# Four instead of six gate and value tiles of the first block in float32, and weight roundings on either engine

## The chip, the cores and the metric

The kernel runs on one core of a Trainium2 chip. The metric is the device time of one execution in microseconds (us). TensorE (PE) multiplies matrices, its weight loads are listed apart as PEld, VectorE is DVE, ScalarE is ACT, GpSimd is POOL, and SP issues the DMAs.

## The reference

A gated linear recurrence runs over 768 tokens of 4 batches with 8 heads of 32 columns (state 16). Its output, 3072 tokens by 256, goes through a gated layer of width 1536:

```python
y[:, :, sl] = y_intra + y_inter                      # chunks of 32 tokens
gate = 1.0 / (1.0 + np.exp(-(x @ w_gate)))           # 3072x256 @ 256x1536
val = x @ w_val
out = (gate * val @ w_out).astype(np.float32)
```

The three weights arrive as 64-bit floats; x, a, B and C as 32-bit floats.

## The kernel before

The tokens are worked on in six blocks of 512 columns (128 tokens of 4 batches). A block has the recurrence (`Scan`, for the first block `FirstUnit`, one unit for each of the 4 batches), then 12 gate and 12 value tiles of 128x512 (`gate`, `value`), then two projections (`proj`). Blocks 4 and 5 are multiplied together in a scheme with sums of operands (`unit`, `paired_proj`).

Weights come in 18 tiles w0 to w17. Even ones of w0 to w11 belong to gates, odd ones to values, each to two widths f: w0 and w1 to f = 0 and 1, w4 and w5 to f = 4 and 5. w12 to w17 are the output weights. `load_w` brings 128 x 1024 words (512 KB) of raw 64-bit floats. `split_w` makes 32-bit floats of them in five steps: a clip (L482, DVE or POOL), a scaled activation (L488, ACT), a shift (L490, DVE), a conversion (L495, ACT) and a sum (L497, POOL). After that the tile is "whole". `part_w` makes two parts of a whole tile: a rounded high part (L513, a copy on ACT) and the difference (L515, DVE or POOL). The parts are made one after the other in the list `order`, tiles that are not "plain" first.

A product in float32 (`thin`, L972) takes the whole weight and x as they are, with two matmuls. A product by parts (L981) takes six matmuls in the faster format, hi x hi, hi x lo and lo x hi for both halves of the contraction, and needs both parts of the weight and of x. The parts of x of the first block come from `parts_of_x` (L888 on ACT, L890 on DVE or POOL, for two halves of the columns). In the first block f = 0 is computed in halves of 256 columns (`halves_of`, L962, float32), f = 1 to 5 with whole 512 columns in float32, and f = 6 to 11 by parts.

The order of the work is written out. `run()` is a planner that runs while the kernel is built: it has one queue for each engine, a fixed cost for each step, the steps' needs, and `DUES`, a list of places: "gate0_1": "122 134" says that the first step of that task has place 122 of 1246 and its second place 134. A letter behind a place (a, d, p) fixes the engine ACT, DVE or POOL of a step that may run on two. Each engine then runs its steps in the planned order. Where the planner expects PE to be idle before 45 us it puts fillers ahead of a product (`keep_warm`, L289, small matmuls with no use): int(0.8 * idle / 0.22 + 0.4) of them. PSUM has three buffers "mm" that products take in turn (a product waits for the release of the third one before it), one "py" that the four first units share, and four banks of the recurrence.

The places of DUES that matter here:

| step | engine | before | after |
|---|---|---|---|
| loads w0, w1, w2, w3, w4 | SP | 3, 31, 43, 58, 76 | 32, 2, 63, 3, 56 |
| loads b0, b3, b1, b2 (B and C of a first unit) | SP | 2, 4, 5, 14 | 4, 5, 17, 24 |
| first transposes `products0_0` of unit 0 | PE | 8 | 23 |
| `spread0`, `spread3`, `spread1`, `spread2` (L741) | PE | 20, 10, 17, 33 | 8, 12, 16, 31 |
| weighing `result0_0` (L695) | DVE | 36 | 47 |
| `result0_2`, fourth step (L820) | PE | 100 | 106 |
| `xparts`, last step (L890) | DVE | 209 | 121 |
| `gate0_1` | PE | 122 | 127 |
| `part4` second step, `part5` second step | DVE | 351, 356 | 145, 185 |
| `gate0_4`, `value0_4` | PE | 168, 179 | 176, 190 |
| `part6` second step, `gate0_6` | DVE, PE | 206, 213 | 202, 212 |
| `part7` second step, `value0_6` | DVE, PE | 218, 223 | 216, 223 |
| `part8`, `gate0_8` | DVE, PE | 236, 240 | 236, 240 |
| `proj0_0` | PE | 283 | 282 |

Of the kernel before, what the change touches and what calls it, by code (L numbers as in the profile page):

```python
# [18 lines left out]
    "": "0 1", "b0": "2", "w0": "3", "b3": "4", "b1": "5", "products0": "6 7 9 13 18", "products0_0": "8 11 28",  # L19
    "spread3": "10 15", "split0": "12 16 19 24 32", "b2": "14", "spread1": "17 23", "spread0": "20 29", "x0": "21",  # L20
    "before0_0": "22p 27", "decays0_3": "25", "x1": "26", "products0_1": "30 34 42", "w1": "31", "spread2": "33 41",
    "x3": "35", "result0_0": "36 46 50 56 63 69", "decays0_0": "37p", "products0_3": "38 44 51", "x2": "39",
    "decays0_1": "40", "w2": "43", "before0_1": "45 47d", "products0_2": "48 55 64", "decays0_2": "49",
    "result0_1": "52 60 66 70 77 82", "early0_0": "53", "before0_3": "54p 57", "w3": "58",
    "result0_3": "59 78 87 91 95 98", "bq1_2": "61", "split1": "62 68 79 85 96", "r": "65", "before0_2": "67p 74p",
    "state0_0": "71", "w5": "72", "result0_2": "73 92 99 100 105 111", "early0_1": "75", "w4": "76",
    "xparts": "80 88d 116 209d", "bq1_0": "81", "half0_0": "83 103 112 117", "state0_1": "84", "w13": "86",
    "w6": "89", "early0_3": "90", "split2": "93 97 102 107 115", "bq1_3": "94", "early0_2": "101", "w7": "104",
    "state0_3": "106", "split3": "108d 119 124 126 139", "bq1_4": "109", "half0_1": "110 118 123 128",
    "state0_2": "113", "w9": "114", "w10": "120", "clip": "121 129 135", "gate0_1": "122 134",  # L30
    "split5": "125 131 136 142 164", "bq1_1": "127", "value0_1": "130 141", "bq1_6": "132",
    "split4": "133 137 143 146 156", "bq1_7": "138", "gate0_2": "140 151", "split13": "144d 150 154 158 177",
    "cq1_1": "145", "value0_2": "147 157", "ap": "148", "bq1_5": "149", "cq1_7": "152", "gate0_3": "153 162",
    "w8": "155", "cq1_4": "159", "split6": "160 165 169 172 183", "value0_3": "161 178",
    "split7": "163d 167 174 181 194", "p": "166", "gate0_4": "168 185", "w11": "170",
    "split9": "171d 175 191 197 233", "cq1_6": "173", "cq1_0": "176", "value0_4": "179 195", "cq1_5": "180",
    "turned1": "182 226", "w12": "184", "cq1_2": "186", "gate0_5": "187 201", "split10": "188 193 203 208 228",
    "cq1_3": "189", "part6": "190 206d", "z": "192", "p1_2": "196", "value0_5": "198 221", "w15": "199",
    "split8": "200d 204 212 216 222", "p1_0": "202", "w17": "205", "p1_3": "207", "w14": "210", "part7": "211 218d",
    "gate0_6": "213 225", "p1_1": "214", "split11": "215 219 238 242 245", "a1_1": "217", "a1_0": "220",  # L40
    "value0_6": "223 231", "bn1": "224", "x1_": "227", "part8": "229 236d", "gate0_7": "230 237",
    "masked1": "232 234", "value0_7": "235 246", "part9": "239 243d", "gate0_8": "240 250",
    "split12": "241d 244 249 253 265", "value0_8": "247 254", "part10": "248 252", "gate0_9": "251 259",
    "split17": "255 262 274 278 282", "value0_9": "256 264", "part11": "257 260d", "split15": "258d 275 284 289 296",
    "gate0_10": "261 268", "split14": "263d 266 270 272 277", "value0_10": "267 276 280d 322", "w16": "269",
    "early1": "271", "gate0_11": "273 281", "value0_11": "279 291 295d 316d",
    "proj0_0": "283 304 337 345 347 350 376", "part17": "285 292", "bq2_4": "286", "decays1": "287 299 300 305 311d",
    "bq2_0": "288", "bq2_6": "290", "bn2": "293", "bq2_2": "294", "part0": "297 308d",
    "proj0_1": "298 325 352 361 364 430 460", "a2_0": "301", "cq2_4": "302", "bq2_5": "303", "bq2_3": "306",
    "cq2_5": "307", "cq2_1": "309", "cq2_6": "310", "part1": "312 336d", "a2_1": "313",  # L50
    "split16": "314 317 320 323 328", "cq2_2": "315", "scan1": "318 332 335 340", "before1": "319d", "bq2_7": "321",
    "cq2_0": "324", "weigh1": "326 329 333 338 344 353 355 357 359", "bq2_1": "327", "cq2_3": "330", "cq2_7": "331",
    "bn3": "334", "part2": "339 341", "state1": "342 349d", "part3": "343 346d", "part4": "348 351d",
    "part5": "354 356d", "part12": "358 360p", "gate1_0": "362 370", "p2_0": "363", "p2_1": "365",
    "value1_0": "366 374 378a 382", "part13": "367 371d", "p2_3": "368", "p2_2": "369", "x2_": "372",
    "gate1_1": "373 381", "part14": "375 377p", "value1_1": "379 387 397 406d", "turned2": "380 384",
    "part15": "383 386", "gate1_2": "385 390", "masked2": "388 394", "value1_2": "389 396 400 426d",
    "decays2": "391 415 434 438 450", "part16": "392 399d", "gate1_3": "393 403", "early2": "395",
    "value1_3": "398 408 417a 422p", "a3_1": "401", "sums0": "402d 409 412p 428d 432p 433 470 482",
    "gate1_4": "404 413", "cq3_0": "405", "cq3_3": "407", "bq3_4": "410", "value1_4": "411 421 425d 445d",  # L60
    "cq3_4": "414", "bq3_0": "416", "gate1_5": "418 427", "bq3_7": "419", "a3_0": "420", "bq3_5": "423",
    "value1_5": "424 431 436 440p", "gate1_6": "429 437", "value1_6": "435 441 444a 499d", "gate1_7": "439 447",
    "value1_7": "442 451 454 462", "cq3_7": "443", "bq3_3": "446", "gate1_8": "448 458", "bq3_1": "449",
    "bq3_2": "452", "cq3_5": "453", "value1_8": "455 463 465a 472p", "before2": "456d", "bn4": "457",
    "decays3": "459 466 492 508 514p", "gate1_9": "461 467", "value1_9": "464 469 471 476",
    "scan2": "468 475 477 495", "gate1_10": "473 479", "weigh2": "474 481 483 488 500 511 513 516 520",
    "value1_10": "478 486 490a 496d", "bq3_6": "480", "gate1_11": "484 493", "cq3_2": "485", "cq3_1": "487",
    "cq3_6": "489", "value1_11": "491 497 501d 503p", "proj1_0": "494 509 517 531 534 561 657", "state2": "498 502d",
    "turned3": "504 515", "p3_0": "505", "p3_1": "506", "p3_3": "507", "x3_": "510", "p3_2": "512",
    "sums1": "518d 523d 524 526d 529d 532 535p 550", "masked3": "519 521", "a4_0": "522", "bq4_3": "525",  # L70
    "bq4_0": "527", "proj1_1": "528 548 560 566 568 593 623", "cq4_4": "530", "cq4_3": "533", "bq4_7": "536",
    "a4_1": "537", "bq4_1": "538", "gate2_0": "539 544", "early3": "540", "bq4_2": "541", "before3": "542p",
    "scan3": "543 549 551 553", "cq4_5": "545", "bq4_4": "546", "cq4_6": "547", "cq4_1": "552", "cq4_0": "554",
    "weigh3": "555 557 562 563 565 576 579 584 587", "state3": "556 559", "cq4_2": "558",
    "sums2": "564 567 569 571p 573p 578 582 592", "bq4_6": "570", "bq4_5": "572", "value2_0": "574 583 585d 589p",
    "cq4_7": "575", "bn5": "577", "p4_1": "580", "gate2_1": "581 588", "value2_1": "586 591 594 597",
    "gate2_2": "590 596", "value2_2": "595 599 600 606", "gate2_3": "598 603", "value2_3": "601 607 611 617p",
    "decays4": "602 622 641 661 671p", "p4_3": "604", "gate2_4": "605 614", "x4_": "608", "turned4": "609 615",
    "p4_2": "610", "value2_4": "612 618 625a 630", "sums3": "613p 627d 629 638d 646p 651 656p 673",
    "gate2_5": "616 624", "masked4": "619 620", "value2_5": "621 628 631a 634p", "gate2_6": "626 633",  # L80
    "value2_6": "632 636 639a 650", "gate2_7": "635 644", "bq5_3": "637", "cq5_5": "640",
    "value2_7": "642 649 653a 665d", "bq5_0": "643", "a5_0": "645", "gate2_8": "647 658", "bq5_2": "648",
    "p4_0": "652", "cq5_1": "654", "value2_8": "655 660 662 667", "gate2_9": "659 664",
    "value2_9": "663 668 669d 692", "gate2_10": "666 672", "value2_10": "670 678 681d 686p", "cq5_3": "674",
    "gate2_11": "675 684", "cq5_7": "676", "early4": "677", "cq5_0": "679", "before4": "680p", "bq5_4": "682",
# [1396 lines left out]
```

## Time and profile before

| | us |
|---|---|
| median of 3 runs | 345.24 (345.18 to 345.71) |
| the profiled execution | 345.54 |
| its span, first to last instruction | 343.7 |
| PE busy | 337.9 (98%) |
| DVE busy | 220.2 (64%) |
| POOL busy | 180.0 (52%) |
| ACT busy | 150.2 (44%) |

The profiled execution's time holds 1.84 us around its span. Matmuls are pipelined, and a duration in the trace overlaps the next one's start; the time that a product takes is read from start to start of successive products.

### The profile page before, as it was taken

To read this page: it belongs to the slowest core of one execution; us is meant where nothing else is said; L and a number is where in the kernel's file an instruction comes from. 1 tells how busy PE (TensorE), PEld (TensorE's weight loads), DVE (VectorE), ACT (ScalarE), POOL (GpSimd) and SP (SyncE) were. 2 spreads that over 40 slices of the span, in tenths; PEclk is the share of its full clock that TensorE was granted. 3 is DMA by queue.
4 is the path that set the end of the run, shared out by engine and by line. 5 is a ranking of instruction groups with operands and counts; after the bars stand their busy time and mean duration, and the time that the engine had idled before them with its cause. 6 is when DMAs were issued, how large, how long until landed. Compare 5 with 4: busy or idle time off the path is not lost.

```text
span 343.7 us, 7948 instructions
## 1 busy us (share of the span) xinstructions
PE 337.9 (98%) x3144; PEld 261.7 (76%) x3144; DVE 220.2 (64%) x377; ACT 150.2 (44%) x277; POOL 180.0 (52%) x181
## 2 busy tenths in 40 slices
PE   8899999999999999999999999999999999999996
PEld 3474587457888888888888888888888888888885
DVE  5889978956879872456666954566064646856221
ACT  4476987124744230136411513361047557645300
POOL 4646265431646434566774545489427885355500
PEclk9999999999999999999999999999999999999999
DMA  6996899871674376476543621108123733220032
GB/s 107 180 352 209 256 272 146 162 132 35 94 159 62 90 109 159 97 139 89 145 100 102 85 76 21 63 3 297 72 36 91 240 89 110 110 61 2 0 58 67
DMA packets 100247, 40.16 MB, mean 117 GB/s; under 512 B 88754, under 2 KB 91826, under 8 KB 99570
## 3 DMA queue, kind: packets, MB, share of 16 engines
q1 hardware_dynamic: 97906, 39.39, 49.3%
q10 hardware_dynamic: 2304, 0.26, 0.5%
q8 instruction: 25, 0.41, 0.5%
q14 instruction: 12, 0.10, 0.1%
HBM read 30.00 MB, written 9.63 MB: 115 GB/s over the span
## 4 chain that ended last, share of the span: by engine, by line
PE 98%; DVE 1%; ACT 0%; issue 0%
PE pg L981 17%; PE pv L981 17%; PE ux L1121 6%; PE acc L1121 6%; PE po L1017 5%; PE po L1013 5%; PE po L1019 5%; PE po L1018 5%; PE acc L1224 5%; PE uz L1121 5%; PE pg L972 2%; PE pv L972 2%; PE po L1251 2%; PE pcb L706 2%; PE pcb L691 2%; PE pcb L647 2%
## 5 line engine op out<-in xcount | busy, mean ns | idle before, releaser
L981 PE MATMUL pg<-xh,w 128*128 128x512 f32 x168 | 59.0, 392 | 0.0
L981 PE MATMUL pv<-xh,w 128*128 128x512 f32 x168 | 58.9, 391 | 0.0
L927 POOL TENSOR_TENSOR h<-g,h 128x512 fp32r<-128x512 f32 x27 | 38.3, 1420 | 24.4 <-ACT h L925 17.2
L921 DVE TENSOR_TENSOR g<-pv,g 128x512 f32<-128x512 f32 x38 | 26.1, 688 | 30.1 <-PE pv L981 29.1
L903 ACT ACTIVATE g<-pg 128x512 f32<-128x512 f32 x47 | 28.0, 596 | 39.4 <-PE pg L981 37.2
L981 PEld LDWEIGHTS pg<-xh,w 128*128 128x128 f32 x168 | 31.5, 188 | 6.7
L981 PEld LDWEIGHTS pv<-xh,w 128*128 128x128 f32 x168 | 31.5, 188 | 6.6
L497 POOL TENSOR_TENSOR wr<-wr 128x512 int32<-128x512 int32 x18 | 20.5, 1143 | 26.8 <-ACT wr L495 13.0
L981 PE MATMUL pg<-xl,w 128*128 128x512 f32 x84 | 32.7, 389 | 0.0
L981 PE MATMUL pv<-xl,w 128*128 128x512 f32 x84 | 32.7, 389 | 0.0
L1017 PE MATMUL po<-h,w 128*128 128x512 f32 x76 | 30.8, 405 | 0.0
L1019 PE MATMUL po<-h,w 128*128 128x512 f32 x76 | 29.6, 390 | 0.0
L1018 PE MATMUL po<-h,w 128*128 128x512 f32 x76 | 29.6, 389 | 0.0
L577 DVE TENSOR_TENSOR_SCAN ab<-ab,delta 128x512 f32<-128x512 f32 x20 | 28.1, 1424 | 0.0
L925 ACT CAST h<-g 128x512 fp32r<-128x512 f32 x26 | 16.0, 619 | 24.2 <-DVE g L921 24.0
L1048 POOL TENSOR_TENSOR c<-c,c 128x512 f32<-128x512 f32 x13 | 17.2, 1326 | 17.9 <-ACT c L1176 9.2
L1048 POOL TENSOR_TENSOR h<-c,h 128x512 fp32r<-128x512 f32 x16 | 21.0, 1323 | 9.4 <-ACT h L1200 9.3
L1048 POOL TENSOR_TENSOR sw<-sw 128x128 f32<-128x128 f32 x36 | 18.9, 535 | 11.2 <-DVE sw L1048 10.2
L1028 DVE STREAM_TRANSPOSE o<-po 128x256 f32<-128x256 f32 x16 | 6.3, 430 | 21.2 <-PE po L1019 19.2
L1200 ACT CAST h<-c 128x512 fp32r<-128x512 f32 x24 | 14.9, 619 | 10.7 <-POOL c L1048 7.1
L981 PEld LDWEIGHTS pv<-xl,w 128*128 128x128 f32 x84 | 15.8, 188 | 3.2
L981 PEld LDWEIGHTS pg<-xl,w 128*128 128x128 f32 x84 | 15.8, 188 | 3.2
(197 smaller groups left out, 733.2 us busy)
## 6 DMA issues: line engine op xcount, KB each, us to landing
w_s<-sp SPq DMA_DIRECT2D x12, 512.0 KB
s<-w_s SPq DMA_DIRECT2D x12, 512.0 KB
ab<-a_z SPq DMA_DIRECT2D x10, 512.0 KB
wr<-in_moe_w_gate_dram SPq DMA_DIRECT2D x6, 512.0 KB
wr<-in_moe_w_val_dram SPq DMA_DIRECT2D x6, 512.0 KB
wr<-in_moe_w_out_dram SPq DMA_DIRECT2D x6, 512.0 KB
xn<-in_x_dram SPq DMA_DIRECT2D x5, 512.0 KB
out_dram<-o SPq DMA_DIRECT2D x144, 16.0 KB
```

Source lines behind the costliest of these rows:

```text
L497: nc.gpsimd.tensor_tensor(out=lw.bitcast(I32), in0=hw.bitcast(I32), in1=lw.bitcast(I32), op=ALU.add)
L577: nc.vector.tensor_tensor_scan(out=t, data0=t, data1=delta.rearrange("p h l -> p (h l)"), initial=0.0, op0=ALU.mult, op1=ALU.add,)
L903: nc.scalar.activation(gs[k, f], pm, AF.Sigmoid)
L921: nc.vector.tensor_tensor(out=g, in0=pm, in1=g, op=ALU.mult)
L927: engines[eng].tensor_tensor(out=hl, in0=g, in1=hh.bitcast(F32), op=ALU.subtract)
L981: nc.tensor.matmul(pm, w[:, part, kt, fs], xx[:, kt], start=(i == 0), stop=(i == 3 * NK - 1))
L1013: nc.tensor.matmul(acc, whole[NF + f // 2][:, f % 2, ms], hs[k, f], start=start, stop=stop)
L1017: nc.tensor.matmul(acc, hi, hh, start=start, stop=False)
L1018: nc.tensor.matmul(acc, hi, hl, start=False, stop=False)
L1019: nc.tensor.matmul(acc, lo, hh, start=False, stop=stop)
L1048: engines[eng].tensor_tensor(out=out, in0=in0, in1=in1, op=op)
L1121: nc.tensor.matmul(out, a[i], b[j], start=start and n == 0, stop=n == 2, skip_group_check=True)
```

## The change

`NPLAIN` falls from 6 to 4: w4 and w5 are no longer plain, so f = 4 and 5 of the first block are multiplied by parts, like f = 6 to 11. Their parts are then made first in `order`, before the tiles of the first block that use them, and not after the first block as now. The rounding copies of `part_w` and of `weight_sums` (L513, L1065) may run on POOL as well as on ACT. All places of DUES are new, for the whole kernel.

```diff
 DUES = {
-    "": "0 1", "b0": "2", "w0": "3", "b3": "4", "b1": "5", "products0": "6 7 9 13 18", "products0_0": "8 11 28",
...
+    "": "0 1", "w1": "2", "w3": "3", "b0": "4", "b3": "5", "products0": "6 7 10 19 25", "spread0": "8 13",
+    "split1": "9 11 28 33 39", "spread3": "12 18", "split3": "14p 21 30 43 50", "x0": "15", "spread1": "16 22",
...
-    NPLAIN = 6
+    NPLAIN = 4
     NWHOLE = 10
...
-    copies = {"dve": nc.vector.tensor_copy, "act": nc.scalar.copy}
+    copies = {"dve": nc.vector.tensor_copy, "act": nc.scalar.copy, "pool": nc.gpsimd.tensor_copy}
...
-        yield step("act", ACT_SB, needs)
+        eng = yield step(("act", "pool"), (ACT_SB, 0.75), needs)
         hw, lw = halves.pop(i)
         hi, lo = parts_of(i)
-        nc.scalar.copy(hi, hw)
+        copies[eng](hi, hw)
...
-        yield step("act", ACT_SB)
+        eng = yield step(("act", "pool"), (ACT_SB, 0.7))
         parts = hp.tile([P, 2, 512], F32R, tag="r1", name=f"sp{i}")
-        nc.scalar.copy(parts[:, 0], t[:, 1])
+        copies[eng](parts[:, 0], t[:, 1])
```

## Rows read from the trace of the kernel before

**Rows 1.** Stretches: length, busy us of PE, PEld, DVE, ACT, POOL; clock, DMA, GB/s.
```profile
0.00:24.36 24.36, 21.75 (x336) 12.98 (x337) 18.03 (x44) 12.77 (x37) 12.23 (x27) 1.00 0.88 203
24.36:34.66 10.30, 10.30 (x25) 4.71 (x24) 9.54 (x14) 6.43 (x11) 6.33 (x7) 1.00 0.72 232
24.36:41.53 17.17, 17.17 (x42) 7.85 (x40) 15.96 (x29) 12.83 (x23) 8.41 (x9) 1.00 0.78 248
200.00:240.00 40.00, 40.00 (x445) 32.91 (x444) 23.12 (x35) 14.63 (x26) 27.08 (x26) 1.00 0.27 90
280.00:320.00 40.00, 40.00 (x179) 33.14 (x178) 25.90 (x40) 23.23 (x42) 21.96 (x20) 1.00 0.25 80
```

**Rows 2.** All waits of PE over the span: us in total, times, longest.
```profile
PE warm L237 <- DVE warm_sb L234: 1.1, 1, 1.1
PE py L706 <- ACT xw L834: 0.5, 1, 0.5
PE pcb L691 <- DVE m L695: 0.5, 1, 0.5
PE py L289 <- ACT xw L834: 0.3, 1, 0.3
PE mm L820 <- DVE sm L724: 0.2, 1, 0.2
```

**Rows 3.** Timeline of PE from 24 to 59 us: start, us, instruction.
```profile
24.36 1.88 PE L972 MATMUL pg<-xw,wr 128*128 128x512 f32 x4
41.53 0.83 PE L289 MATMUL pg<-eye 128*128 128x128 f32 x6
42.12 0.48 PE L981 MATMUL pg<-xh,w 128*128 128x512 f32 x1
43.59 0.38 PE L289 MATMUL pv<-eye 128*128 128x128 f32 x2
43.73 0.48 PE L981 MATMUL pv<-xh,w 128*128 128x512 f32 x1
45.20 0.40 PE L981 MATMUL pg<-xh,w 128*128 128x512 f32 x1
49.30 0.39 PE L981 MATMUL pv<-xh,w 128*128 128x512 f32 x1
58.83 10.46 PE L1013 MATMUL po<-h,wr 128*128 128x512 f32 x24
```

**Rows 4.** Timeline of DVE, 40 to 49 us: parts of weights (L515) and x (L890).
```profile
40.59 0.68 DVE L515 TENSOR_TENSOR w<-wr,w 128x512 fp32r<-128x512 f32 x1
41.19 0.68 DVE L890 TENSOR_TENSOR xl<-xw,xh 128x512 fp32r<-128x512 f32 x1
48.01 0.69 DVE L515 TENSOR_TENSOR w<-wr,w 128x512 fp32r<-128x512 f32 x1 [0.51 <-issue]
```

**Rows 5.** Timeline of PE, 5 to 25 us: transposes, visits, fillers, halves.
```profile
5.95 0.30 PE L756 MATMUL pt<-eye,bn 128*128 128x128 f32 x1
6.19 1.02 PE L741 MATMUL pa<-apart,of_unit 128*128 128x512 f32 x2
12.63 0.24 PE L706 MATMUL py<-m,xn 64*32 64x64 f32 x1
13.28 0.33 PE L756 MATMUL pt<-eye,bn 128*128 128x128 f32 x1
17.03 0.71 PE L289 MATMUL py<-eye 128*128 128x128 f32 x4 [0.27 <-ACT xw L834]
18.53 1.14 PE L962 MATMUL pgv<-xw,wr 128*128 128x256 f32 x4
19.60 0.45 PE L820 MATMUL mm<-cd,sm 128*64 128x64 f32 x8
20.64 0.71 PE L289 MATMUL mm<-eye 128*128 128x128 f32 x4
21.28 0.45 PE L820 MATMUL mm<-cd,sm 128*64 128x64 f32 x8
21.66 2.86 PE L962 MATMUL pgv<-xw,wr 128*128 128x256 f32 x12
```

**Rows 6.** Timeline of DVE, 6 to 30 us.
```profile
6.89 0.43 DVE L482 TENSOR_SCALAR wr<-wr 128x512 f32<-128x512 f32 x1 [1.98 <-DMA wr<-in_moe_w_gate_dram]
7.25 1.22 DVE L744 TENSOR_TENSOR_SCAN ab<-pa,delta 128x512 f32<-128x512 f32 x1
11.38 0.69 DVE L695 TENSOR_TENSOR m<-pcb,ab 128x512 f32<-128x512 f32 x1
25.74 1.26 DVE L482 TENSOR_SCALAR wr<-wr 128x512 f32<-128x512 f32 x1
29.37 2.59 DVE L1307 TENSOR_TENSOR_SCAN a<-a,az 32x768 f32<-32x768 f32 x1
```

**Rows 7.** SP: issue of the first weight load.
```profile
2.58 0.67 SPq L468 DMA_DIRECT2D wr<-in_moe_w_gate_dram  x1
```

**Rows 8.** Groups by line and shape, whole span.
```profile
L513 ACT CAST w<-wr 128x512 fp32r<-128x512 f32 x18 | 11.6, 658 | 4.9 <-DVE w L515 3.9 <-POOL w L515 1.0
L515 POOL TENSOR_TENSOR w<-wr,w 128x512 fp32r<-128x512 f32 x6 | 8.5, 1423 | 10.5 <-ACT w L513 10.5
L482 DVE TENSOR_SCALAR wr<-wr 128x512 f32<-128x512 f32 x18 | 10.6, 597 | 2.0 <-DMA wr<-in_moe_w_gate_dram 2.0
```

**Rows 9.** POOL at the start: the one copy of 128x512; and its sum at 25.61.
```profile
2.09 0.61 POOL L257 COPY delta<-eye 128x512 f32<-128x512 f32 x1 [0.78 <-DVE eye L255]
25.61 1.11 POOL L497 TENSOR_TENSOR wr<-wr 128x512 int32<-128x512 int32 x1
```

230 rows, old and new, of the table DUES are left out of this document.

## The prediction

> **What bounds the kernel now.** I read the stretches first, then the waits of PE, then its timeline. The stretches show PE busy from end to end behind 24.36 us (the reader sees the length and the busy time equal), and idle for 24.36 - 21.75 = 2.6 us before it; the granted clock is 1.00, the 2.4 GHz level, everywhere [rows 1]. The waits say the same from the other side: PE waited five times, 2.6 us together [rows 2]. So from the first float32 gate tile at 24.36 [rows 3] the program is one unbroken queue on PE. What shortens that queue shortens the kernel one for one as long as no operand comes late, and what moves its start moves the end. The other engines matter through operands that PE would wait for. They are tightest in the first block, where DVE is busy 9.54 of 10.30 us [rows 1].
>
> **The products.** The ten float32 products of f = 1 to 5 run from 24.36 to 41.53 [rows 3]: 1.717 us each. The last ten by parts run from 45.20 to 58.83 [rows 3]: 1.363 each. Four change kind: 4 x (1.363 - 1.717) = -1.42 us on PE.
>
> **The fillers at the seam.** Where PE goes over to parts it runs six fillers from 41.53 to 42.12 and two from 43.59 to 43.73 [rows 3], 0.59 + 0.14 = 0.73 us. They stand where the plan expected x's low part, which DVE ends at 41.87 [rows 4], and the parts of w7. After the change that step of x has place 121, ahead of the first gate. If the parts of w4 to w7 are on time no filler is needed: -0.73. If the plan expects as much idle time at the new seam they move there: 0. I take -0.73 and count late parts by themselves.
>
> **Parts earlier.** w4 and w5 get their parts ahead of gate0_4 and value0_4: for each an ACT copy of 0.66 us [rows 8] and a DVE difference of 0.68 [rows 4]. Behind the first block as much falls away, where nothing was late. With the gate at 24.36 the seam comes at 24.36 + 6 x 1.717 = 34.66 and gate0_6 at 34.66 + 4 x 1.363 = 40.11, against 42.12 now. So DVE must end w6's difference, now at 41.27 [rows 4], some 1.2 us earlier. Queued ahead of it on DVE from the first gate on are, if the flexible steps stay there: 2 differences and its own at 0.68, 12 clips and shifts at 0.42 (the short row [rows 6]) or 0.60 (the mean [rows 8]), four gate-value products at 0.69 (taken as the differences are), one scan over a at 2.59 [rows 6], and 0.8 for the halves: 13.2 or 15.4 us. The step of x, four of w13 and the transposes of chunk 1 now stand elsewhere. There are 40.11 - 24.36 = 15.75 us. DVE's own waits now take 17.17 - 15.96 = 1.2 us of this stretch [rows 1]. So PE stalls between 0 (13.2 + 1.2) and 0.9 (15.4 + 1.2 - 15.75). I take 0.4, about the middle. What is late next is w9: its difference ends at 48.70 [rows 4], value0_8, the first to use it, starts at 49.30 [rows 3], 0.6 us of slack at today's pace.
>
> **POOL as a place for roundings.** The trace has no rounding on POOL. From below its price is the one copy of this size, 0.61 us, from above POOL's difference with the same operands, 1.42; ACT needs 0.66 [rows 8, 9]. POOL was busy 8.41 of 17.17 us [rows 1] and has room. The other price is on DVE: a clip took 1.26 us while POOL's sum ran from 25.61 to 26.72, against 0.43 alone [rows 6, 9], so 0.8 us went to one POOL instruction. The copies without a fixed engine ahead of gate0_6 are three (w4, w5, w6). Three times 0.8 on DVE is 2.4; zero is the other end, if they stay on ACT or fall beside DVE work that reads PSUM. I take 0.2 for PE, near the lower end, as the rows above leave DVE some cover and ACT has the shorter queue. The Trainium skill, "SBUF — State Buffer", section "Who interferes with whom", says that DVE and GpSimd share a pair of ports under an exclusive lock and that the later one blocks fully; the long clip agrees with it. By that rule every rounding on POOL would stop a clip or shift for its whole length; this is the third rival.
>
> **The head.** The start of the queue is the other term, and the new places change it throughout. Now the transposes of unit 0 run at 5.95 and its weighing on DVE at 11.38 [rows 5, 6]. The new order loads w1 and w3 ahead of B and C and lets PE spread three units first. A scan begins 7.25 - 6.19 = 1.06 us after its spread [rows 5, 6], so the first at about 7.0; the transposes wait for a buffer "mm" that the second scan releases, 1.22 us each [rows 6]: 9.4. Behind them come ACT's copies, two more scans and a few short steps on DVE, and unit 0's weighing ends at about 13.9, 1.8 us later than now. By then the other units are further than now. What PE has left up to the first gate is four visits of 0.65 (12.63 to 13.28), four of 0.38 (21.28 to 21.66), halves of 1.07 and 2.70, and 1.2 for transposes and products of units 1 and 2 [rows 5]: 9.1 us. Now the same pieces take from 12.63 to 24.36, 11.7 us, with eight fillers and waits among them [rows 2, 5]. So the new first gate lies between 13.9 + 9.1 = 23.0 and 13.9 + 11.7 = 25.6, that is -1.4 to +1.2. I take 24.1, -0.3, just below the middle, since three units ready at once should need fewer waits.
>
> **Behind the first block** PE's work is the same piece for piece, and PE has no wait there now [rows 1, 2]. The order is new for every engine; I take 0, with a few tenths open either way.
>
> **Sum**, against the profiled execution's 345.54 us (span 343.7 and 1.84 around it): -1.42 - 0.73 + 0.4 + 0.2 - 0.3 = -1.85, so 343.7. The median of the runs lies 0.3 below that execution: 345.24 - 1.85 = 343.4.
>
> **Rivals.** (1) The weights keep their pace: parts come as late as now, and the queue gains only the least slack, 0.6 us at w9: 344.6. For it: DVE at 93% ahead of the seam [rows 1]. Against: x's late part has moved away, and POOL has room. (2) Slower, by a late start: B and C of every unit stand behind 1 MB of weights. The first weight load was issued at 2.58 and its clip began, when it had landed, at 6.89 [rows 6, 7], 4.3 us. If each of the two delays B and C by half of that, unit 0 is ready 4.3 us later than 5.95, 0.9 past the 9.4 at which its buffer is free, and x, with a third load ahead, up to another 1.0. With today's waits the gate then starts at 26.5 to 27.5. The other terms give -1.55, so it decides from 24.36 + 1.55 = 25.9 on; the time is 345.8 to 346.8, I say 346.4. For it: all of PE's waits are in the head now [rows 2]. Against: the loads land while DVE is at its scans. (3) POOL's roundings lock DVE: of the 2.4 us above, less the 0.6 already counted, 1.7 shows: 345.1. For it the long clip, against it that only three copies are free to move.
>
> **Chances.** Forecast 0.55 (its own range 342.3 to 344.3), rival 1 0.2, rival 2 0.15, rival 3 0.1. A measurement can tell from no change here about 0.2%, 0.7 us: faster is below 344.55, slower above 345.93. The forecast is all faster; rival 1 gives 0.12 faster and 0.08 same; rival 2 0.13 slower and 0.02 same; rival 3 0.02 faster, 0.06 same, 0.02 slower. Together 0.69, 0.16 and 0.15. The range runs from 342.0 (no stall, gate 1.1 early: -1.42 - 0.73 - 1.1 = -3.25) to 345.4, with rivals 1 and 3 in it; the late start is left out.
>
> **What would show it.** In the changed profile: six whole float32 products of 1.72 us and sixteen by parts of 1.36 in the first block; the first gate tile between 23.0 and 25.6; gate0_6 at about 40 without fillers ahead of it, or else a wait or fillers there (rival 1; with long clips beside copies on POOL, rival 3); the first projection at about 57 instead of 58.83 [rows 3]; no wait of PE behind that. A first gate behind 25.9 makes the prediction wrong, and so does any wait of PE behind 60 us that adds up to more than a microsecond.

## The result, and the profile after

| | before | after |
|---|---|---|
| median, us | 345.67 (22 runs, 345.18 to 345.97) | 347.84 (22 runs, 346.16 to 351.01) |
| ratio, with its 95% interval | | 1.0067 (1.0055 to 1.0078) |
| profiled execution; its span | 345.54; 343.7 | 348.59; 346.8 |
| first float32 gate | 24.36 | 27.29 |
| first gate to first projection | 34.47 | 34.13 |
| first projection to the end of the span | 284.87 | 285.38 |

The change makes the kernel 0.7% slower; forecast were 343.4 us and a range up to 345.4. Its executions also spread over 4.9 us, those of before over 0.8. Of the 3.1 us that the span gained, 2.93 lie ahead of the first gate, -0.34 between it and the first projection, 0.51 behind. The profiled execution after lies 0.75 us above its kernel's median, so the terms below add up to 3.1 us where the medians differ by 2.2. Ratios leave out executions more than 1.5% above the fastest of their kernel, which medians and ranges keep (one each of e3, e10 and e12). (Lines of the changed kernel are numbered one lower: L971 is L972 of before.)

The stretches of the kernel after, as in [rows 1]: length, busy us of PE, PEld, DVE, ACT, POOL, each with its rows, then the clock, DMA share and GB/s.

```profile
0.00:18.90 18.90, 17.15 (x219) 9.96 (x219) 14.00 (x32) 9.39 (x28) 12.15 (x26) 1.00 0.86 167
0.00:24.50 24.50, 21.90 (x344) 13.64 (x345) 17.79 (x45) 12.85 (x37) 12.78 (x26) 1.00 0.90 207
0.00:27.28 27.28, 24.05 (x354) 15.60 (x355) 20.08 (x48) 13.96 (x39) 14.20 (x27) 1.00 0.92 223
27.29:61.42 34.13, 33.84 (x134) 24.00 (x133) 27.82 (x49) 25.09 (x44) 15.29 (x16) 1.00 0.87 197
61.42:346.80 285.38, 282.22 (x2689) 226.78 (x2687) 170.37 (x278) 108.98 (x189) 158.60 (x145) 1.00 0.43 96
```

The same view of the kernel before, for the two stretches that [rows 1] does not have:

```profile
24.36:58.83 34.47, 34.47 (x122) 22.27 (x121) 30.17 (x56) 27.29 (x48) 17.72 (x18) 1.00 0.92 230
58.83:343.70 284.87, 281.68 (x2689) 226.42 (x2687) 171.98 (x279) 110.17 (x193) 150.05 (x137) 1.00 0.42 96
```

Keep the counts in mind: up to the first gate PE ran 354 matmul rows, 336 before [rows 1]. All waits of PE in the kernel after, which answer to [rows 2]:

```profile
PE pgv L961 <- issue: 1.4, 1, 1.4
PE warm L236 <- DVE warm_sb L233: 1.1, 1, 1.1
PE mm L819 <- issue: 0.6, 1, 0.6
PE pv L980 <- DVE w L514: 0.3, 1, 0.3
PE py L705 <- DVE m L694: 0.2, 1, 0.2
```

The two largest new ones name no operand: "issue". Where they lie is seen in PE's timeline of the kernel after (start, us, instruction, rows, idle time before it), to be read against [rows 3, 5]:

```profile
14.12 0.24 PE L705 MATMUL py<-m,xn 64*32 64x64 f32 x1 [0.21 <-DVE m L694]
15.93 0.71 PE L288 MATMUL py<-eye 128*128 128x128 f32 x4
17.63 0.49 PE L288 MATMUL mm<-eye 128*128 128x128 f32 x2
18.05 0.39 PE L819 MATMUL mm<-cd,sm 128*64 128x64 f32 x5
19.01 0.33 PE L819 MATMUL mm<-cd,sm 128*64 128x64 f32 x3 [0.58 <-issue]
19.93 0.71 PE L288 MATMUL mm<-eye 128*128 128x128 f32 x4
23.06 0.71 PE L961 MATMUL pgv<-xw,wr 128*128 128x256 f32 x2
25.14 2.32 PE L961 MATMUL pgv<-xw,wr 128*128 128x256 f32 x10 [1.37 <-issue]
27.29 1.02 PE L971 MATMUL pg<-xw,wr 128*128 128x512 f32 x2
38.98 1.05 PE L288 MATMUL pv<-eye 128*128 128x128 f32 x8
45.37 0.60 PE L288 MATMUL pv<-eye 128*128 128x128 f32 x4
```

The reader sees PE stop in the middle of a group of equal small products (after five of eight rows of L819) and between the two matmuls of one half product, which read the same two tiles. The stops stand at matmul rows 219 and 344 of the stretches above. At the seam there are now 12 rows of fillers (8 before), 0.81 + 0.36 = 1.17 us from start to next start.

### The profile page after: what moved, and what is told of

The parts are those of the page before. It is cut to its first block, busy times and chain, and to the rows that moved or that the text cites. A ratio compares the mean times of both kernels' runs of the same rounds, so it can differ in the third digit from the quotient of the medians.

```text
span 346.8 us, 8004 instructions
## 1 busy us (share of the span) xinstructions
PE 340.1 (98%) x3174; PEld 266.4 (77%) x3174; DVE 218.3 (63%) x375; ACT 148.0 (43%) x272; POOL 188.1 (54%) x188
## 4 chain that ended last, share of the span: by engine, by line
PE 97%; issue 1%; DVE 1%; ACT 0%; DVEq 0%
PE pg L980 17%; PE pv L980 17%; PE ux L1120 6%; PE acc L1120 5%; PE po L1016 5%; PE po L1012 5%; PE po L1018 5%; PE po L1017 5%; PE acc L1223 5%; PE uz L1120 5%; PE po L1250 2%; PE pcb L705 2%; PE pcb L690 2%; PE pcb L646 2%; PE pv L971 1%; PE pg L971 1%
## 5 line engine op out<-in xcount | busy, mean ns | idle before, releaser
L980 PE MATMUL pv<-xh,w 128*128 128x512 f32 x176 | 61.9, 392 | 0.3 <-DVE w L514 0.3
L980 PE MATMUL pg<-xh,w 128*128 128x512 f32 x176 | 62.1, 394 | 0.0
L926 POOL TENSOR_TENSOR h<-g,h 128x512 fp32r<-128x512 f32 x27 | 37.4, 1391 | 11.7 <-ACT h L924 9.3
L980 PEld LDWEIGHTS pv<-xh,w 128*128 128x128 f32 x176 | 33.0, 188 | 7.6 <-DVE w L514 0.7
L980 PEld LDWEIGHTS pg<-xh,w 128*128 128x128 f32 x176 | 33.0, 188 | 7.4 <-issue 0.2
L924 ACT CAST h<-g 128x512 fp32r<-128x512 f32 x33 | 20.4, 620 | 34.6 <-DVE g L920 34.5
L980 PE MATMUL pg<-xl,w 128*128 128x512 f32 x88 | 34.3, 390 | 0.0
L980 PE MATMUL pv<-xl,w 128*128 128x512 f32 x88 | 34.3, 389 | 0.0
L576 DVE TENSOR_TENSOR_SCAN ab<-ab,delta 128x512 f32<-128x512 f32 x20 | 29.4, 1474 | 0.0
L1047 POOL TENSOR_TENSOR c<-c,c 128x512 f32<-128x512 f32 x14 | 19.4, 1389 | 17.1 <-DVE c L1161 9.3
L1047 POOL TENSOR_TENSOR sw<-sw 128x128 f32<-128x128 f32 x33 | 16.6, 510 | 15.1 <-DVE sw L1047 14.6
```

The lines of the kernel that those rows point to most:

```text
L576: nc.vector.tensor_tensor_scan(out=t, data0=t, data1=delta.rearrange("p h l -> p (h l)"), initial=0.0, op0=ALU.mult, op1=ALU.add,)
L924: copies[eng](hh, g)
L926: engines[eng].tensor_tensor(out=hl, in0=g, in1=hh.bitcast(F32), op=ALU.subtract)
L980: nc.tensor.matmul(pm, w[:, part, kt, fs], xx[:, kt], start=(i == 0), stop=(i == 3 * NK - 1))
L1047: engines[eng].tensor_tensor(out=out, in0=in0, in1=in1, op=op)
```

## The experiments

Theory A is that the new order of the head costs the time: A1, PE's gaps belong to numbers of its instruction stream, where the next block of instructions isn't there yet; A2, operands are late there. Theory B is that the parts of the weights set the pace at the seam. Medians of before on the same chips were 345.26 (e1 to e4), 345.30 (e5 to e8), 345.43 (e9, e10), 345.33 (e11) and 345.52 (e12).

**One half of the order at a time.** e1 is the kernel before (six float32 tiles) with the new order up to the first gate; e2 the kernel after with the old one.

```diff
 DUES = {          # e1: in before.py
-    steps up to gate0_1 in the order of before
+    steps up to gate0_1 in the order of after, the rest as before
 DUES = {          # e2: in after.py
-    steps up to gate0_1 in the order of after
+    steps up to gate0_1 in the order of before, the rest as after
```

> The kernel before (six f in float32, roundings on ACT) with the changed kernel's order up to the first gate tile only; the old order from there on. Theory A (the loss is the head: PE's start of the queue comes about 3 us later): first gate at about 27.3 us as in the changed kernel, time before + 2.9 - 0.7 (no late parts at the seam, since the weights had longer) = about 347.8 us, with a spread of some us between runs. Theory B (the loss is at the seam, where parts by weights come late): no loss here, 345 us or less.

> The changed kernel (four f in float32) with the old order up to the first gate tile, the new order from there on. Theory B or the prediction's third step (parts of w4 to w7): the first gate is at 24.4 again. If parts are on time, 345.6 - 1.4 - 0.7 = 343.5 us. If the weights' pace is the bound, PE waits or runs fillers at the seam (f = 4 and 5) for about 3 to 4 us, the first projection is no earlier than 58.8, and the time is 346 to 347.5. Theory A alone (only the head was wrong) says 343.5 to 344.5.

e1 took 350.98, ratio 1.0163 (1.0146 to 1.0179); e2 348.18, 1.0079 (1.0064 to 1.0095). PE's timeline of e1, then of e2:

```profile
26.24 2.32 PE L961 MATMUL pgv<-xw,wr 128*128 128x256 f32 x10 [2.19 <-issue]
28.39 1.88 PE L971 MATMUL pg<-xw,wr 128*128 128x512 f32 x4
47.85 0.72 PE L980 MATMUL pg<-xh,w 128*128 128x512 f32 x2 [1.65 <-DVE w L514]
```
```profile
34.58 1.05 PE L288 MATMUL pg<-eye 128*128 128x128 f32 x8
36.87 2.62 PE L288 MATMUL pv<-eye 128*128 128x128 f32 x22
```

The new head brings the gap along into the old kernel, at the same product; the time is 3 us above what A said, with 2.1 us of waits for weights at the seam and the first gate 1.1 us later than A had it. With the old head the gap at the half product is gone (0.28 us are left at row 219) and the first gate is at 24.28. But of the 3.0 us saved there 2.1 go at the seam, with 30 rows of fillers (3.2 us from start to next start): the first projection is at 60.49, and the time 0.7 us above what B said.

**No fillers; other numbers of rows.** e3 is the kernel after without any filler. e4 (before) and e5 (after) have the same warm-up columns in eleven matmuls instead of three, 16 rows more. e6 drops after's fillers ahead of the first gate (13 matmuls, not 16) and puts 26 rows of 32 columns into the warm-up instead.

```diff
-FILL, MORE, FILL_T, COLD = 0.8, 0.4, 0.22, 45.0      # e3
+FILL, MORE, FILL_T, COLD = 0.0, 0.0, 0.22, 45.0
-WARM = (4, 4, 3)                                     # e4, e5
+WARM = (1, 1, 1, 1, 1, 1, 1, 1, 1, 1, 1)
-for _ in range(int(FILL * idle[0] / FILL_T + (0.9 if first_y[0] else MORE))):   # e6
+for _ in range(int(FILL * idle[0] / FILL_T + (0 if first_y[0] else MORE))):
-idle[0] = start - free["pe"] if eng == "pe" and start < COLD else 0.0      # e6
+idle[0] = start - free["pe"] if eng == "pe" and 27.0 < start < COLD else 0.0
+for _ in range(13):
+    nc.tensor.matmul(warm[:, :32], warm_sb, warm_sb[:, :32], start=True, stop=True)
```

> The changed kernel without any filler matmul. Theory A1 (PE's gaps in the head lie at fixed instruction numbers, 219 and 344 matmul rows, where the next block of instructions has not arrived): the 26 filler rows ahead of the second gap are gone, so that place moves into the float32 gates, where an instruction lasts 0.2 us, and the 1.4 us gap ahead of the halves goes; 1.5 to 2.5 us less than the changed kernel, about 345.5 to 346, and less spread. Theory A2 (the gaps are operands that come late): the gap stays at the halves, fillers turn into waits, 347 to 348 us.

> The kernel before with the same warm-up columns in 11 matmuls of 128 columns in place of 3 (16 more matmul rows and 16 more weight loads ahead of everything, nothing else). Theory A1: the block's end that fell at row 345, in the float32 gates, now falls at old row 329, among the halves of f = 0, after the fast small matmuls; a gap without a data wait appears there at about 22 to 24 us, the time rises by 0.3 to 1.5 us and its spread grows. Theory A2: no change, 345.6 within 0.3.

> The kernel after, with 16 more matmul rows in the warm-up, ahead of everything (the same columns cut into eleven short matmuls instead of three). Theory A1 (PE's gaps without a shown wait stand at numbers of its instruction stream, where the next block of instructions is not there yet): the gaps, now at matmul rows 219 and 344 from the start, stay at these numbers, so they move 16 rows back in the work: the first (0.58 us) out of the group L819 x5 into the products L690 ahead of it, the second (1.37 us) out of the second half product to just ahead of the first, at about 21.6. The time changes little (347 to 349) if their sizes stay. Theory A2 (an operand is late there): the gaps stay at the same instructions of the work, 0.58 inside L819 and 1.37 inside the second half product, and the time stays at 347.8.

> The kernel after without its 16 fillers ahead of the first gate, and with 13 matmuls of 32 columns in the warm-up, so that every piece of work from the second unit's visit on keeps its number in PE's stream to within a few rows; the fillers at the seam stay. Theory A1: the gaps come back at the same rows as in the kernel after (inside L819 and inside the second half product) though no filler is left; the first gate lies at 25.5 to 26.5, only the fillers' own time earlier than 27.29, and the time is 346.2 to 347.2. Theory F (the fillers themselves hold the head up, the gaps are a by-product of the time they take): no gaps above 0.5 us, first gate at 24.3 to 24.7 as without any filler, time 345.2 to 345.8.

e3 took 346.67, 1.0042 (1.0023 to 1.006): first gate 24.35, the gap at the halves gone, 328 rows ahead of the gate; the time is 0.7 us above what A1 said, and a gap of 1.00 us stands at row 1743. e4 took 345.89, 1.0023 (1.0011 to 1.0036): rise and spread (2.2 us) are as A1 said, but its profiled run, at 345.48 one of the fastest, does not show the gap. PE came to row 344 there at 22.66, just as its block was ready: its packet (such packets are shown below) ended at 21.24, 2.4 us sooner than in the kernel before. e5 took 354.48, 1.0274 (1.025 to 1.0297), and e6 352.64, 1.0214 (1.0182 to 1.0247). The sizes that I expected of e5 and e6 were far too small. The places were right, but for e6's second gap, which did not come. Stretches and timeline of e5:

```profile
0.00:17.60 17.60, 15.93 (x219) 11.32 (x220) 13.45 (x31) 8.92 (x28) 11.99 (x25) 1.00 0.85 168
0.00:24.00 24.00, 19.50 (x345) 14.10 (x346) 16.94 (x41) 11.40 (x34) 13.03 (x26) 1.00 0.85 199
24.60:28.60 4.00, 3.95 (x17) 2.69 (x17) 0.69 (x4) 0.99 (x3) 0.00 (x0) 0.57 1.06 359
18.00 0.45 PE L690 MATMUL pcb<-bct 32*64 32x128 f32 x9 [0.79 <-issue]
24.63 0.21 PE L715 MATMUL mm<-xn,bd 64*32 64x64 f32 x1 [3.06 <-issue]
```

With 16 rows put in at the start the gaps stay at rows 219 and 345 and so fall into other work: into the products L690 and into the last row of a visit. That is A1's forecast to the row, and A2 falls. Behind the 3.06 us the granted clock was 0.57 over 4 us, so mostly the 1.2 GHz level, which costs again. The first gate came at 30.48, 3.2 us later than in the kernel after. Behind the first projection e5 needs 288.1 us, 2.75 more than the kernel after; two later gaps make 2.5 of these:

```profile
84.61 0.27 PE L646 MATMUL pcb<-ct,sm 32*64 32x64 f32 x2 [1.54 <-issue]
202.77 0.50 PE L1017 MATMUL po<-h,w 128*128 128x512 f32 x1 [1.00 <-issue]
```

e6, its stretch up to the gap and the gap:

```profile
0.00:22.00 22.00, 17.49 (x218) 10.43 (x219) 14.23 (x32) 9.48 (x28) 12.94 (x26) 1.00 0.90 195
23.27 0.45 PE L821 MATMUL mm<-cd,sm 128*64 128x64 f32 x8 [3.08 <-issue]
```

Row 218, without a filler in sight. (The 26 small rows also delayed the first scans by 3.6 us, and behind the gap the clock was 0.60 over 4 us, so e6 says nothing on the fillers' own time.)

**What ends a gap.** The trace has a DMA queue of kind "instruction". The kernel after, 22.50 to 23.00 us, then the whole span (packets, MB, share of 16 engines):

```profile
q8 instruction: 1, 0.02, 13.9%
q8 instruction: 25, 0.41, 0.5%
```

Each of its packets has 0.41 MB / 25 = 16 KB; the one above took 0.139 x 16 x 0.5 = 1.11 us. Narrow stretches give each packet's start to 0.05 us, and every gap ends 1.3 to 1.5 us behind the end of one:

| kernel | matmul rows before the gap | packet starts, ends | PE goes on | behind it | gap |
|---|---|---|---|---|---|
| after | 219 | 16.05, 17.56 | 19.01 | 1.45 | 0.58 |
| after | 344 | 22.60, 23.71 | 25.14 | 1.43 | 1.37 |
| e1 | 344 | 23.85, 24.95 | 26.24 | 1.29 | 2.19 |
| e5 | 219 | 15.05, 16.54 | 18.00 | 1.46 | 0.79 |
| e5 | 345 | 22.10, 23.20 | 24.63 | 1.43 | 3.06 |
| e6 | 218 | 20.70, 21.92 | 23.27 | 1.35 | 3.08 |
| e9 (below) | 1744 | 159.50, 160.59 | 162.10 | 1.51 | 1.37 |

The other gaps without an operand that the traces show (of 0.28 to 1.65 us: one each in e2, e7, e10, e11 and e12, two in e3 and the two later ones of e5) end 1.4 to 1.6 us behind a packet too.

In the kernel before the packets start as late, at 15.25 and 22.55, and at row 219 PE waits only 0.1 us. But there PE has 336 rows ahead of the gate, and row 344 comes behind the second float32 product, at 24.36 + 2 x 1.717 = 27.8. The block is there at 23.65 + 1.4 = 25.1, and nothing waits. In the kernel after PE is at row 344 at 23.77 and waits until 25.14. In all fourteen traces the packet for that row starts 2.5 (e6) to 5.2 us (e3) behind row 219. With 1.0 to 1.3 us for the packet and 1.3 to 1.5 behind it, I estimate that the 125 rows must keep PE busy for 5 to 8 us to hide the next block. In the kernel after they held 4.75 us of work (19.01 to 23.77), in the kernel before 9.7 (18.12 to 27.80).

The Trainium skill, "Runtime: NRT & Kernel Launch", section "Instruction fetch mechanics", says that instructions come in blocks of 16 KiB (256 instructions), that the next one is fetched while one runs, and that crossing a border is mostly hidden. The size agrees: 16 KB a packet, and 125 matmul rows with as many weight loads between the borders. That it is hidden does not: up to 3.1 us showed.

**The fillers at the seam.** e7 (after) and e8 (before) plan no filler behind 30 us.

```diff
-FILL, MORE, FILL_T, COLD = 0.8, 0.4, 0.22, 45.0
+FILL, MORE, FILL_T, COLD = 0.8, 0.4, 0.22, 30.0
```

> The kernel after without the 6 filler matmuls (12 rows) at the seam alone (ahead of value0_4 and value0_6); the head is as in the kernel after. Theory B1 (those fillers fill time that the weights' parts need anyway): PE waits there instead, for a difference of a weight (L514), 0.8 to 1.6 us in all, the stretch from the first gate to the first projection stays at 33.8 to 34.3, and the time at 347.3 to 348. Theory B2 (the plan expects waits that the chip does not have): the stretch falls to 32.5 to 33.0, and the time to 346.0 to 346.8.

> The kernel before without its 4 filler matmuls (8 rows, 0.73 us) at the seam. Theory B1: waits of PE for the parts of x or of w7 take their place, the time stays within 0.2 of 345.3. Theory B2: the time falls by 0.4 to 0.7, to 344.6 to 344.9, and the first projection starts at 58.1 to 58.4 instead of 58.83.

e7 took 346.29, 1.0027 (1.0013 to 1.0041); e8 344.60, 0.998 (0.9971 to 0.9988), the best of all kernels here. Timeline and stretch of e7, then the stretch of e8:

```profile
25.26 2.32 PE L961 MATMUL pgv<-xw,wr 128*128 128x256 f32 x10 [1.65 <-issue]
27.41 1.02 PE L971 MATMUL pg<-xw,wr 128*128 128x512 f32 x2
27.41:60.09 32.68, 32.40 (x122) 22.66 (x121) 28.33 (x49) 24.95 (x44) 15.44 (x16) 1.00 0.91 201
```
```profile
24.80:58.62 33.82, 33.80 (x113) 21.29 (x112) 30.86 (x56) 26.92 (x48) 17.84 (x18) 1.00 0.87 212
```

34.13 - 32.68 = 1.45 us of the stretch went with the fillers, and only 0.3 of waiting is there (for a weight's difference, as in the kernel after): the plan had filled idle time that the chip does not have (B2). In e8 the stretch fell from 34.47 to 33.82. Its first gate came at 24.80 in the profiled run, the slowest of its 12, so that one shows no gain; that e8 is faster rests on its 12 runs.

**The head gap taken away.** e9 is e7 without the eight fillers ahead of unit 0's first visit, where PE waits for the weighing anyway; e10 is e2 without fillers at the seam.

```diff
-idle[0] = start - free["pe"] if eng == "pe" and start < COLD else 0.0      # e9
+idle[0] = start - free["pe"] if eng == "pe" and 15.0 < start < 30.0 else 0.0
-FILL, MORE, FILL_T, COLD = 0.8, 0.4, 0.22, 45.0                            # e10, on e2
+FILL, MORE, FILL_T, COLD = 0.8, 0.4, 0.22, 30.0
```

> The kernel after without the seam's fillers (as in e7) and also without the 8 filler matmuls (16 rows) that stand ahead of unit 0's first visit, where PE waits for DVE's weighing at 14.12 anyway; the 5 fillers behind that visit stay. Theory A1: the work of PE moves 16 rows forward in its instruction stream, the second block border (row 344) now falls behind the first float32 gate, whose products of 1.7 us give the block time to come, and the first border into the third visit; so the gap of 1.4 to 1.65 us at the half product goes and that of 0 to 0.6 shrinks: first gate at 25.0 to 25.9 instead of 27.4, time 344.2 to 344.9. Theory F (the fillers' own time holds the head up): the dropped ones ran where PE waits anyway, so the first visit stays at 14.1, the gate at 27.0 to 27.5, the time at 346.3.

> The kernel after with the order of before up to the first gate (as in e2) and without any filler at the seam, where e2 ran 30 rows of them (3.7 us). Theory B1 (with the old head the weights' parts of f = 4 and 5 are late on the chip too): PE waits for a difference (L514) at the seam in their place, 1.5 to 3 us, first projection behind 59, time 345.5 to 347.5. Theory B2 (only the plan's costs are too long there): little wait, first gate at 24.3 to 24.8 and the stretch to the first projection 32.7 to 33.3 as in e7, first projection at 57.0 to 58.0, time 343.2 to 344.4, below before's.

e9 took 347.02, 1.007 (1.0042 to 1.0099); e10 349.35, 1.0112 (1.0083 to 1.0142). Stretches and timeline of e9:

```profile
0.00:24.81 24.81, 22.12 (x338) 13.58 (x339) 18.81 (x47) 13.88 (x39) 14.03 (x27) 1.00 0.94 221
24.82 1.88 PE L971 MATMUL pg<-xw,wr 128*128 128x512 f32 x4
24.82:56.94 32.12, 32.12 (x121) 22.73 (x120) 28.75 (x51) 25.22 (x44) 15.03 (x17) 1.00 0.86 201
56.94 7.03 PE L1012 MATMUL po<-h,wr 128*128 128x512 f32 x16
0.00:161.50 161.50, 158.04 (x1744) 115.12 (x1744) 119.30 (x210) 75.64 (x144) 94.05 (x98) 1.00 0.71 149
162.10 0.34 PE L646 MATMUL pcb<-ct,sn 32*64 32x64 f32 x8 [1.37 <-issue]
162.10:166.00 3.90, 3.90 (x41) 3.17 (x42) 2.34 (x7) 1.78 (x3) 0.00 (x0) 0.66 0.18 27
```

The head came out as A1 said: the first visit stays (14.02), no gap is left, the gate is 2.6 us earlier than in e7. (e11 and e12 below have the same head; in theirs 0.63 and 0.31 us are left at row 218, and the gate is at 25.39 and 25.14.) The first projection starts at 56.94, 1.9 us ahead of before. But the time was missed by over 2 us: from there to the end e9 needs 288.3 us, 3.4 more than before. A gap of 1.37 at row 1744 stands in it, with the clock at 0.66 over the 3.9 us behind; by that clock 1.3 us are lost again, so that the two make an estimated 2.7 of the 3.4. e3 and e10, whose work lies otherwise, have a gap at row 1743 (1.00 and 0.87 us). In e10 B1's wait came, the old head leaves the weights late; its time is 1.9 us above what B1 said. Its wait and stretch:

```profile
PE pv L980 <- DVE w L514: 2.0, 1, 2.0
0.00:163.80 163.80, 158.88 (x1743) 114.45 (x1743) 121.54 (x209) 74.57 (x142) 97.90 (x101) 1.00 0.68 147
```

**The gap near 160 us.** e11 puts before's order behind e9's first block. e12 is e9 with four float32 products cut into halves, which gives every row from f = 4 on the number that it has in e7.

```diff
 DUES = {          # e11, on e9
-    steps from proj0_0 on in the order of after
+    steps from proj0_0 on in the order of before
-for kt in range(NK):                                                       # e12, on e9
-    nc.tensor.matmul(pm, ..., xw[0][:, kt], ...)
+for c in ([slice(0, 256), slice(256, 512)] if f in (2, 3) else [slice(0, 512)]):
+    for kt in range(NK):
+        nc.tensor.matmul(pm[:, c], ..., xw[0][:, kt, c], ...)
```

> As e9 up to the first projection (after's products and order, no fillers at the seam or ahead of unit 0's first visit), behind it the order of before. Ahead of the first projection PE has then 458 matmul rows against 456 in the kernel before, so the borders of instruction blocks fall where they fall in the kernel before, to within two rows, in the visits of the recurrence too. Theory A1 (what e9 lost behind the first block, 3.4 us, is the same kind of gap at a visit near 160 us, 1.4, and the lower clock behind it): no gap above 0.3 us in the visits between 140 and 200 us, first projection at 56.9, 284.9 from there to the end as in the kernel before, so 343.7, and a spread of its runs near that of before. Theory C (the earlier first block is given back by something else behind it, such as weights or parts that are late for blocks 1 and 2): a wait of PE for an operand between 57 and 200 us, 345 to 347.

> As e9 (no fillers at the seam or ahead of unit 0's first visit), with the four float32 products of f = 2 and 3 cut into halves of 256 columns: 16 more matmul rows behind the first gate, so that every row from f = 4 on has the number that it has in e7. Cost of the cut: 8 more pairs of short rows, 0.3 us at most (twelve rows of 256 columns took 2.7 us, six of 512 would take 2.6). Theory A1 (e9's loss behind the first block is a block border at row 1744, in the middle of a recurrence visit, with the clock's fall behind that gap): gate at 24.8 as in e9, first projection at 57.0 to 57.3, no gap near 160 as in e7, time 343.5 to 344.3, below before. Theory C (an earlier first block is given back behind it whatever the row numbers are): a gap or a wait of 1 us or more between 60 and 200 us, time 346 to 347.5.

e11 took 349.56, 1.0107 (1.0087 to 1.0126): the two orders do not fit, and PE waited 2.0 us for x's parts of the next block and 1.2 for a weight (theory C). It has no gap between 140 and 200 us, but its time lies above both forecasts and tells little beyond that. e12 took 346.23, 1.0026 (1.0008 to 1.0045), its profiled run 346.26. Waits and stretch of e12:

```profile
PE pv L981 <- DVE w L514: 1.4, 1, 1.4
PE py L705 <- issue: 0.3, 1, 0.3
25.14:59.05 33.91, 32.51 (x137) 25.80 (x136) 29.04 (x51) 25.39 (x44) 16.32 (x17) 1.00 0.85 206
```

The gap near 160 us is gone, as A1 said: from 59.05 to the end it takes 344.5 - 59.05 = 285.4 us, as in the kernel after and not e9's 288.3. The time was missed by 2 us through B: in that run PE waited 1.4 us for a weight's difference behind a load that landed late (DVE's clip waited for it until 48.00, in e9 until 46.51). With an early gate the weights have little slack: waits for them show in e10 and e12, though not in the profiled run of e9. No kernel with four float32 tiles has a median below that of the kernel before; the nearest are e12 and e7.

## Why the prediction was wrong

**The head, -0.3, measured +2.93: the step that failed.** Its first half held. Unit 0's weighing was to end at about 13.9, and the first visit started at 14.12; so rival 2, which had a late gate by late operands, has the right place and the wrong cause. The visit's start is 1.5 us later than in the kernel before (12.63), of which 1.3 were foreseen; the work behind it was to make up for them and took 1.4 us more instead. From there I took 9.1 us of work, and up to 11.7 with today's fillers and waits. Measured were 13.17: 9.1, fillers of 0.64 + 0.42 + 0.64 = 1.70, gaps of 0.58 + 1.37 = 1.95, and 0.4 of other small delays. With the fillers alone the gate would have come at 25.3 at the latest, inside the range that I gave; e9 has these same fillers and no gap, and its gate is at 24.82. What I had not counted is that PE's own instructions can be late. The trace of before shows no such wait, since its 344th row lies among slow products; what speaks for it there, the instruction queue and the row counts, I did not read.

**The fillers at the seam, -0.73, measured about +0.8.** The step named two ends, "if the parts of w4 to w7 are on time no filler is needed: -0.73. If the plan expects as much idle time at the new seam they move there: 0", and I chose by the chip what the plan decides. (The six and two are rows, two to a filler matmul.) The plan put 12 rows there, and leaving them out gained 1.45 us (e7), against 0.65 in the old kernel (e8): 0.8 more.

**The products, -1.42: right. Late parts, +0.4: right in size, by luck.** In e9, without fillers at the seam or waits, the stretch is 32.12; 6 x 1.717 + 16 x 1.363 is 32.11. In e7 it is 32.68 against 34.47, -1.79; the terms -1.42 - 0.73 + 0.4 give -1.75. But the wait in it is 0.3, for w10 or w11 near 57.7 and not at gate0_6, and I had reckoned with a gate at 24.36: the gate that came 2.9 us later gave the weights that time. Where the gate is early the waits were 2.0 (e10, gate at 24.17), 1.4 (e12, 25.14) and none (e9, 24.82). So rival 1's pace of the weights did not bind in the kernel after because its head was late, and is a part of why the gain did not come back when the gaps went.

**POOL's roundings, +0.2, measured nothing in the first block.** The uses of L512 on POOL in the kernel after (durations, first and last start), and the mean of its group:

```profile
L512 POOL CAST w<-wr x3: 645/647/847, 70.3 to 90.5; 128x512 fp32r<-128x512 f32 x3
L512 POOL CAST w<-wr 128x512 fp32r<-128x512 f32 x3 | 2.1, 713 | 0.0
```

All three lie behind the first block, at the lower end of the price that I gave (0.61 to 1.42). Rival 3 played no part. (Its sum has a slip: 2.4 less 0.6 is 1.8, not 1.7.)

**Behind the first block, 0, measured +0.51**, within the few tenths left open in that profiled run. But the spread of 4.9 us over the runs was not foreseen. Gaps at later borders, as in e3, e5, e9 and e10, would make it; the profiled run of the kernel after has none, so this is argued and not shown.

**What stays open.** What sets the start of an instruction packet was not tried. In the time between row 219 and the start of the next packet the DMA share was 0.78 to 1.08, and it does not order the delays: 2.5 us with 1.05 (e6), 2.6 with 0.78 (e4), 5.2 with 0.81 (e3). Whether fewer loads would bring the packet sooner is not known. Nor are e7's and e8's gains free of the border's effect behind the first block, since 12 and 8 rows fewer move every later border too.

## What to carry to other kernels

When a trace has waits that name no operand ("issue") in the middle of equal small products, count rows up to them in two kernels: equal numbers in different work mean instruction blocks, not data. In a stretch of many tiny matmuls every added row, fillers above all, can pull a block border ahead of the slow products that would hide it, so count rows as well as microseconds. Fillers planned from a cost table are work like any other: leave them out once and see whether a wait takes their place.

## What the runs showed of the hardware

- 16 rows more ahead of everything took the kernel after from 347.84 to 354.48 us (e5), though the same columns were multiplied.
- A gap of 3.06 us was followed by a granted clock of 0.57 over 4 us, one of 1.37 near 160 us by 0.66 over 3.9; behind the 1.37 of the kernel after and the 2.19 of e1, where large float32 products followed, the clock stayed at 1.00.
- The first two instruction packets of a kernel, 16 KB each, took 1.0 to 1.6 us, and PE went on 1.3 to 1.5 us behind their end where it waited for them.
- POOL rounded a tile of 128x512 in 0.65 us twice and in 0.85 once, ACT in 0.66 [rows 8].
